# An attention and feed-forward kernel: V products of two key tiles in one batch, feed-forward products in small segments over double turns

## The chip, the core and the metric

The kernel runs on one NeuronCore of a Trainium2 chip. The metric is device time in microseconds (us) of one execution, the median of several runs. Five engines work side by side, each with its own instruction stream, and wait for each other by semaphores: TensorE (PE, matrix products; its weight loads are listed apart as PEld), VectorE (DVE), ScalarE (ACT), GpSimd (POOL) and SyncE (SP, which issues DMAs here).

## What is computed

The input is one sequence of 2048 tokens of width 512. After a layer norm, full attention with 32 heads of width 16 runs beside a gated feed-forward block of width 1792, and the two are joined:

```
xn = layernorm(x)
q, k, v = split(xn @ wqkv)                  # 32 heads of 16
p = softmax(q @ k.T / sqrt(16))             # 2048 x 2048 for each head
s = (p @ v) @ wo
h = (xn @ w_gate) * (xn @ w_up)
out = x + s * silu(h @ w_down)
```

All of it is in fp32. Most products are split in a high and a low part (fp32r), which gives three products for each one.

## The kernel before, in words

**Units and turns.** The attention is cut into 32 units `i` (8 groups of 4 heads, times 4 chunks of 512 queries). A unit takes 16 turns, one for each tile `kt` of 128 keys, so that there are 512 turns. A turn handles 4 heads `j`. For each head, `expo` (L568 to L578) makes the scores `t` (keys by queries, 128x512, one PSUM bank), and ScalarE takes their exponential into an SBUF tile `e`. Beside it `score` (L542) makes scores `s` of a later unit (queries by keys, `LEAD` = 21 turns ahead), whose row maxima VectorE takes (`mx`, L552). The maxima go back into `qs` by DMA and are subtracted by the product `t` itself.

**Couples.** `t` of head j uses the lower or the upper 64 rows of the PE array (its first row is 64 * (j % 2)), and `s` of head j ^ 1 the other 64 rows. The two run at the same time on the two halves; this text calls them a **couple**. A turn has four couples.

**V products.** `pv` (L580) multiplies the four `e` tiles with 32 columns of V each. The four products take all 128 rows and one column group of 32 each, and run at the same time; being fp32, each is carried out in two passes (8 matmul records for 4 products). This text calls what stands together a **batch**. Before, the batch of a turn is issued at the end of the next turn. All 16 turns of a unit add into one bank `pv`, which `finish` transposes and divides by its last column.

**Filler.** What PE does beside the attention comes from a generator, `filler` and later `ending`: products of q and k (`p`), gate and up (`g`, `u`), down (`y`) and the output (`z`). They come as `pair`s (L229): two outputs in two banks, one product on the lower 64 rows and one on the upper 64 rows at each step. This text calls one such step a **pair step**. One call of `pair` (a **call** below) makes 12 or 15 pair steps, exchanges the halves (between them ScalarE reads one word of the second bank, `look`, L251, for which the second half waits), and makes as many again. Calls of 24 pair steps are 13 of `p`, 56 of `g` and `u` and 8 of `y`; calls of 30 are 16 of `y`. That is 2328 pair steps (`SLOTS`), and the output's come on top. `Filler.part` (L758) is called once in each turn, after the second couple. It spreads each half of a call evenly over a number of turns that `spread` (L771) gives out of `FFN_ROUNDS` = 484, so that a turn has 4, 5 or 6 pair steps in one piece.

A turn on PE is thus: couple, couple, 4 to 6 pair steps, couple, couple, batch.

**Buffers.** PSUM has 8 banks (`BUFS`): 2 for `t` (tag st), 3 for `s`, 1 for `pv`, 2 for the filler (misc). So the third `t` may start only when the first one's exponential has read its bank: couple n waits for the exponential of couple n - 2, and for the maximum of couple n - 3. `e` has 12 buffers. The order on PE, ACT and DVE is the order of the code (`manual_schedule`); only DMAs and POOL are placed by the framework. `soon(n, f)` issues f after n more couples.

Of the kernel before, what the change touches and what calls it, by code (L numbers as in the profile page):

```python
# [21 lines left out]
NT = S // P  # L22
# [6 lines left out]
VW = DH + 1  # L29
VCOLS = (H - 1) * VW + 32  # L30
THIRDS = [range(0, 5), range(5, 10), range(10, 14)]
LEAD = 21
FFN_ROUNDS = 484
SLOTS = 24 * (NC * (NG // 2 - 1) + 1) + 36 * NF * NC
SPLIT_ROUNDS = 4
EBUFS = 12
# [10 lines left out]
def body(ctx, tc, x, wqkv, wo, wg, wu, wd, out):  # L47
    nc = tc.nc
# [3 lines left out]
    def dma(dst, src):  # L52
        nc.sync.dma_start(dst, src)
# [22 lines left out]
    V = keep.tile([P, NT, VCOLS], F32, name="V")  # L76
# [42 lines left out]
    def etile():  # L119
        return ep.tile([P, 512], F32, name="e", bufs=EBUFS)  # L120
# [398 lines left out]
    def load_q(i):  # L519
        g, c = divmod(i, NC)  # L520
        QS[i] = q = keep.tile([P, 2, 512], F32R, name="qs", bufs=3)
        MX[i] = keep.tile([P, 4, 4, 4], F32, name="mx", bufs=2)
        for e in range(2):
            dmar(q[64 * e:64 * e + KB], two(QD[g // 2][c][64 * (g % 2):64 * (g % 2) + 64], e))

    def load_k(g, cs=range(NC)):
        heads = slice(64 * (g % 2), 64 * (g % 2) + 64)
        for e in range(2):
            k = ks[g % 2][64 * e:64 * e + KB]
            if g < 2:  # L530
# [14 lines left out]
    def score(i, r, j):  # L545
        kc, t = divmod(r, 4)
        b, pr = 64 * (j % 2), j // 2
        k = ks[(i // NC) % 2]
        o = psum("s", f"s{i}_{r}_{j}")
        nc.tensor.matmul(o, QS[i][b:b + KB, pr, t * P:(t + 1) * P],  # L550
                         k[b:b + KB, pr, kc * 512:(kc + 1) * 512], start=True, stop=True)
        nc.vector.tensor_reduce(MX[i][:, j, t, kc:kc + 1], o, axis=AX.X, op=OP.max)  # L552
# [18 lines left out]
    def expo(i, kt, j):  # L571
        b, pr = 64 * (j % 2), j // 2
        k = ks[(i // NC) % 2]
        o = psum("st", f"t{i}_{kt}_{j}")
        nc.tensor.matmul(o, k[b:b + KR, pr, kt * P:(kt + 1) * P], QS[i][b:b + KR, pr], start=True, stop=True)  # L575
        e = etile()
        nc.scalar.activation(e, o, AF.Exp, scale=DH ** -0.5)  # L577
        return e  # L578

    def pv(i, kt, es):  # L580
        g = i // NC
        if kt == 0:
            fst["pv"] = psum("pv", f"pv{i}")
        for j in range(4):
            h0 = (4 * g + j) * VW
            nc.tensor.matmul(fst["pv"][32 * j:32 * j + 32], V[:, kt, h0:h0 + 32], es[j],  # L586
                             start=kt == 0, stop=kt == NT - 1)

    def finish(i):

        g, c = divmod(i, NC)
        tr = keep.tile([P, 16, 32], F32, name="tr", bufs=1)
        tn = tr.rearrange("p b e -> p (b e)")
        nc.vector.transpose(tn, fst["pv"])
# [121 lines left out]
    def filler(wq0):  # L716
        yield from proj_pair(0, [(wq0, 0, 2), (wq0, 0, 3)])
        for m in range(1, NG // 2):
            wk, wq = qk_weights(m, 1), qk_weights(m, 0)
            for c in range(NC):  # L720
                yield from proj_pair(m, [(wk, 1, c), (wq, 0, c)])
                if m == 1 and c:
                    after = fst["high"].ins.name
                    for n, src in enumerate((xh, xl)):
                        put = nc.sync.dma_start(XD[c][n].bitcast(F32), src[c].bitcast(F32))
                        tc.add_manual_dep(put.ins, after, BEHIND, reason="not before the first exponentials")
                if m == NG // 2 - 1 and c == NC - 2:
# [8 lines left out]
    heads = []  # L736

    def step_small(q):
        if q and next(q[0], 1):
            q.pop(0)  # L740

    class Filler:


        def __init__(self, gen, rounds):
            self.gen, self.rounds = gen, rounds
            self.left = self.parts = 0
            self.done = False

        def fetch(self):  # L750
            v = next(self.gen, self)
            if v is self:
                self.done = True
            elif v:
                self.left, self.parts = v[1], self.rounds(v[1])

        def part(self):
            if not self.left and not self.done:  # L758
                self.fetch()
            if self.left:  # L760
                n = -(-self.left // self.parts)
                for _ in range(n):
                    next(self.gen)
                self.left -= n
                self.parts = max(1, self.parts - 1)
                if not self.left:
                    self.fetch()

    cum = [0]

    def spread(n):  # L771
        a = cum[0]
        cum[0] += n
        return max(1, round(cum[0] * FFN_ROUNDS / SLOTS) - round(a * FFN_ROUNDS / SLOTS))

    prev = None
    with tc.manual_schedule(engines=ORDERED):
        with banks_of(EARLY_BUFS):
            fil = Filler(filler(early()), spread)
        ctx.enter_context(banks_of(BUFS))  # L780
        for n in range(NU * 16):
            now[0] = n
            i, kt = divmod(n, 16)
            g, c = divmod(i, NC)
            si, sr = divmod(n + LEAD, 16)
            if kt == 8 and i + 2 < NU:
                load_q(i + 2)
            if kt == 0 and g + 1 < NG and c == 1:
# [24 lines left out]
        run(finish(NU - 1))  # L813
        flush()
        last_heads()
        while fil.left or not fil.done:
            now[0] += 1
            prepare()
            fil.part()
            flush()  # L820
    ffp.close()

# [15 lines left out]
```

## Time and profile before

| | |
|---|---|
| time, median of 3 runs | 1816.01 us (1815.8 to 1816.85) |
| span of the profiled execution, first to last instruction | 1815.7 us; of its own time the record gives no more than this span |
| POOL busy | 580.7 us (32%) |
| PEld busy (weight loads, beside PE) | 991.1 us (55%) |
| DMA, mean over the span | 80 GB/s |

The span lies 0.3 us below the median of the runs. A busy share says little by itself here: PE's matmul records overlap, so that what a stretch costs is read from the starts of its records in the timeline, which is an answer of the trace that lists instructions in order of time: start, duration, engine, line, operation, output<-inputs, shapes, and how many records are merged. In square brackets stand the idle time of that engine before it and what ended it.

### The profile page before, as it was taken

What the parts mean: (1) busy time and instruction counts of PE and PEld (TensorE: products, weight loads), DVE (VectorE), ACT (ScalarE), POOL (GpSimd) and SP (SyncE); (2) the same over time, 40 slices, a digit from 0 to 9 for tenths busy, and PEclk for the clock granted to TensorE, in tenths of its full rate; (3) what the DMA queues carried; (4) which work ended last, traced back from release to release, by engine and by line L of the source; (5) the groups of instructions that cost most, each with busy time, mean ns of one, the idle gap of its engine ahead of it and who ended that gap; (6) DMA issues with size and microseconds to landing.
All of it is one profiled execution on the core that took longest, in us unless ns stands there. A gap on an engine that the chain in (4) does not pass through costs nothing.

```text
span 1815.7 us, 34194 instructions
## 1 busy us (share of the span) xinstructions
PE 1794.1 (99%) x13568; PEld 991.1 (55%) x13568; DVE 1474.4 (81%) x2456; ACT 1238.3 (68%) x2365; POOL 580.7 (32%) x647
## 2 busy tenths in 40 slices
PE   8899999999999999999999999999999999999998
PEld 5565555555555555555555555555555555555555
DVE  8488888888888888888888888888888888888832
ACT  5137676777776767777777777776767767767674
POOL 5321332431331325232132441431315323223441
PEclk9899999999999999999999999999999999999999
DMA  5424633520222122321115220411125111111352
GB/s 198 112 54 163 225 118 115 148 62 22 68 64 54 49 86 80 80 55 42 39 42 131 69 63 22 94 52 33 52 79 126 46 40 57 34 48 45 110 156 79
DMA packets 117227, 145.72 MB, mean 80 GB/s; under 512 B 12620, under 2 KB 74060, under 8 KB 114380
## 3 DMA queue, kind: packets, MB, share of 16 engines
q1 hardware_dynamic: 117068, 143.55, 27.7%
q8 instruction: 106, 1.74, 0.4%
q14 instruction: 53, 0.43, 0.1%
HBM read 95.94 MB, written 47.45 MB: 79 GB/s over the span
## 4 chain that ended last, share of the span: by engine, by line
PE 94%; DVE 2%; DMA 2%; POOL 1%; issue 0%; ACT 0%; SPq 0%; POOLq 0%; ACTq 0%; DVEq 0%
PE pv L586 27%; PE t L575 21%; PE s L550 11%; PE y L243 6%; PE u L243 5%; PE g L243 4%; PE u L247 4%; PE g L247 4%; PE y L247 3%; PE p L243 3%; PE v L224 2%; PE p L247 2%; PE z L243 1%; PE z L247 1%; DMA wdr<-in_wd_dram 1%; PE p L224 0%
## 5 line engine op out<-in xcount | busy, mean ns | idle before, releaser
L552 DVE TENSOR_REDUCE mx<-s 128x1 f32<-128x512 f32 x2048 | 1311.7, 683 | 268.5 <-PE s L550 162.7
L577 ACT ACTIVATE e<-t 128x512 f32<-128x512 f32 x2048 | 1111.9, 596 | 427.0 <-PE s L550 236.3
L550 PE MATMUL s<-ks,qs 48*128 48x512 f32 x2048 | 700.1, 427 | 10.0 <-DMA ks<-KD 8.8
L575 PE MATMUL t<-qs,ks 50*128 50x512 f32 x2048 | 705.2, 426 | 0.3 <-ACT e L577 0.3
L575 PEld LDWEIGHTS t<-qs,ks 50*128 50x128 f32 x2048 | 347.2, 185 | 499.4 <-ACT e L577 474.0
L586 PE MATMUL pv<-e,V 128*32 128x512 f32 x4096 | 545.7, 605 | 0.0
L550 PEld LDWEIGHTS s<-ks,qs 48*128 48x128 f32 x2048 | 337.4, 185 | 33.9 <-issue 12.9
L138 POOL CAST w0h<-w0r 128x512 fp32r<-128x512 f32 x60 | 36.7, 612 | 407.2 <-PE u L243 257.9
L586 PEld LDWEIGHTS pv<-e,V 128*32 128x32 f32 x4096 | 81.0, 108 | 156.5 <-issue 147.3
L352 POOL CAST dh<-wdr 128x512 fp32r<-128x512 f32 x56 | 33.8, 614 | 182.9 <-PE y L247 92.4
L247 PE MATMUL u<-fh,w0h 64*128 64x512 f32 x224 | 88.2, 394 | 0.1
L247 PE MATMUL y<-dh,hh 64*128 64x512 f32 x224 | 88.1, 393 | 0.0
L243 PE MATMUL u<-fh,w0l 64*128 64x512 f32 x224 | 88.0, 393 | 0.0
L243 PE MATMUL g<-fh,w1l 64*128 64x512 f32 x224 | 87.8, 392 | 0.0
L247 PE MATMUL g<-fl,w1h 64*128 64x512 f32 x224 | 87.8, 392 | 0.0
L243 PE MATMUL u<-fh,w0h 64*128 64x512 f32 x224 | 87.7, 392 | 0.0
L247 PE MATMUL g<-fh,w1h 64*128 64x512 f32 x224 | 87.7, 392 | 0.0
L243 PE MATMUL g<-fh,w1h 64*128 64x512 f32 x224 | 87.7, 391 | 0.0
L243 PE MATMUL u<-fl,w0h 64*128 64x512 f32 x224 | 87.6, 391 | 0.0
L243 PE MATMUL g<-fl,w1h 64*128 64x512 f32 x224 | 87.6, 391 | 0.0
L243 PE MATMUL y<-dh,hh 64*128 64x512 f32 x224 | 87.6, 391 | 0.0
L243 PE MATMUL y<-dl,hh 64*128 64x512 f32 x224 | 87.5, 391 | 0.0
(250 smaller groups left out, 2885.1 us busy)
## 6 DMA issues: line engine op xcount, KB each, us to landing
w1r<-in_wg_dram SPq DMA_DIRECT2D x56, 256.0 KB
w0r<-in_wu_dram SPq DMA_DIRECT2D x56, 256.0 KB
wdr<-in_wd_dram SPq DMA_DIRECT2D x56, 256.0 KB
qs<-QD SPq DMA_DIRECT2D x64, 192.0 KB
ks<-KD SPq DMA_DIRECT2D x12, 768.0 KB
KD<-hl SPq DMA_DIRECT2D x16, 512.0 KB
QD<-hl SPq DMA_DIRECT2D x16, 512.0 KB
OD<-tr SPq DMA_DIRECT2D x31, 256.0 KB
```

Source lines behind the costliest of these rows:

```text
L138: cast = nc.gpsimd.tensor_copy(hi, raw)
L224: nc.tensor.matmul(o, l(d), r(d), start=k == d == 0, stop=k == 2 and d == ND - 1)
L243: nc.tensor.matmul(outs[k], l[LOWER], r[LOWER], start=k == 0 and n == 0, stop=(stop or k == 0) and n == len(low) - 1, skip_group_check=k == 1)
L247: nc.tensor.matmul(outs[1 - k], l[UPPER], r[UPPER], start=k == 0 and m == 0, stop=(stop or k == 0) and m == len(high) - 1, skip_group_chec ...
L352: nc.gpsimd.tensor_copy(dh[:, i], raw)
L550: nc.tensor.matmul(o, QS[i][b:b + KB, pr, t * P:(t + 1) * P], k[b:b + KB, pr, kc * 512:(kc + 1) * 512], start=True, stop=True)
L552: nc.vector.tensor_reduce(MX[i][:, j, t, kc:kc + 1], o, axis=AX.X, op=OP.max)
L575: nc.tensor.matmul(o, k[b:b + KR, pr, kt * P:(kt + 1) * P], QS[i][b:b + KR, pr], start=True, stop=True)
L577: nc.scalar.activation(e, o, AF.Exp, scale=DH ** -0.5)
L586: nc.tensor.matmul(fst["pv"][32 * j:32 * j + 32], V[:, kt, h0:h0 + 32], es[j], start=kt == 0, stop=kt == NT - 1)
```

## The change

It does three things. `pv` takes the `e` tiles of two turns and issues 8 products in one batch (16 matmul records). The batch moves from the end of a turn to the middle of every even turn, after its second couple. And the filler is dealt out in segments: five in each double turn, one after the last couple of the even turn and one after each couple of the odd turn. A call of `pair` as a whole (both halves, 24 or 30 pair steps) gets a whole number of double turns, 2 to 4 out of `PHASES` = 242, and so 10, 15 or 20 segments. `finish` is issued two couples after the batch. Banks and buffers stay as they were.

```diff
-FFN_ROUNDS = 484
+PHASES = 242
+SEGS = 5
...
-    def pv(i, kt, es):
+    def pv(i, es):
         g = i // NC
-        if kt == 0:
-            fst["pv"] = psum("pv", f"pv{i}")
-        for j in range(4):
...
+        for kt, four in es:
+            if kt == 0:
+                fst["pv"] = psum("pv", f"pv{i}")
+            for j in range(4):
...
+                k, self.half = v
+                if not self.segs:
+                    self.total = self.left = self.half * (2 - k)
+                    self.segs = self.all = SEGS * self.phases(self.total)
...
+        def segment(self):
+            if not self.half and not self.done:
+                self.fetch()
+            if not self.segs:
+                return
+            self.segs -= 1
+            n = self.left - self.total * self.segs // self.all
+            self.left -= n
+            while n and not self.done:
+                if not self.half:
+                    self.fetch()
+                    continue
+                m = min(n, self.half)
+                for _ in range(m):
                     next(self.gen)
-                self.left -= n
-                self.parts = max(1, self.parts - 1)
-                if not self.left:
+                n -= m
+                self.half -= m
+                if not self.half:
                     self.fetch()
...
-        return max(1, round(cum[0] * FFN_ROUNDS / SLOTS) - round(a * FFN_ROUNDS / SLOTS))
+        return max(1, round(cum[0] * PHASES / SLOTS) - round(a * PHASES / SLOTS))
...
+    def products():
+        pv(*before)
+        if before[1][-1][0] == NT - 1:
+            i = before[0]
+
+            def rest():
+                heads.append(finish(i))
+                step_small(heads)
+            soon(2, rest)
...
-            es = []
+            four = []
+            es.append((kt, four))
             for j in range(4):
-                es.append(expo(i, kt, j))
+                four.append(expo(i, kt, j))
...
-                    fil.part()
+                if kt % 2 == 0 and j == 1 and before:
+                    products()
+                if kt % 2 or j == 3:
+                    fil.segment()
...
-            if prev is not None:
-                pv(*prev)
-                if prev[1] == NT - 1:
-                    heads.append(finish(prev[0]))
-                    step_small(heads)
-            prev = i, kt, es
-        pv(*prev)
+            if kt % 2:
+                before, es = [i, es], []
+        pv(*before)
+        flush()
...
-        while fil.left or not fil.done:
+        while not fil.done:
```

The order on PE around key tile 8 of unit 17, in names unit_tile_head: before, the last two couples of tile 7, the batch of tile 6, then the first two couples of tile 8 and the first of its pair steps.

```order
L575 MATMUL t17_7_2_14293<-qs_12780,ks0_132 128x512
L550 MATMUL s18_12_3_14297<-ks0_132,qs_13553 128x512
L575 MATMUL t17_7_3_14300<-qs_12780,ks0_132 128x512
L550 MATMUL s18_12_2_14304<-ks0_132,qs_13553 128x512
L586 MATMUL pv17_14019<-e_14198,V_137 32x512
...
L575 MATMUL t17_8_0_14315<-qs_12780,ks0_132 128x512
L550 MATMUL s18_13_1_14319<-ks0_132,qs_13553 128x512
L575 MATMUL t17_8_1_14322<-qs_12780,ks0_132 128x512
L550 MATMUL s18_13_0_14326<-ks0_132,qs_13553 128x512
L243 MATMUL g2_1_14283<-fl_13981,w1h_13991 128x512
```

After, on PE in the same place: the last couple of tile 7, a segment of one pair step, both couples of tile 8, the batch of tiles 6 and 7 (8 rows), and the third couple of tile 8.

```order
L576 MATMUL t17_7_3_14266<-qs_12772,ks0_132 128x512
L551 MATMUL s18_12_2_14270<-ks0_132,qs_13548 128x512
L244 MATMUL u2_0_14057<-fh_13997,w0l_13354 128x512
L248 MATMUL g2_0_14056<-fh_13997,w1l_13348 128x512
L576 MATMUL t17_8_0_14298<-qs_12772,ks0_132 128x512
L551 MATMUL s18_13_1_14302<-ks0_132,qs_13548 128x512
L576 MATMUL t17_8_1_14306<-qs_12772,ks0_132 128x512
L551 MATMUL s18_13_0_14310<-ks0_132,qs_13548 128x512
L588 MATMUL pv17_14033<-e_14192,V_137 32x512
...
L576 MATMUL t17_8_2_14321<-qs_12772,ks0_132 128x512
```

Before, a batch or a piece of filler of 4 to 6 pair steps stood between a couple and the second one after it. Now from `t17_7_3` to `t17_8_1`, two couples on in the same bank, there is one couple and one pair step.

On ACT before, the rows from tile 7 to tile 8 of the same unit: the copy `g` and the copy `hh` of the filler stand between exponentials of couples that have a batch or a piece of filler behind them.

```order
L577 ACTIVATE e_14205<-t17_6_1_14203 128x512
L346 ACTIVATE g_14222<-g2_0_14038 128x512
L577 ACTIVATE e_14243<-t17_6_2_14241 128x512
L577 ACTIVATE e_14251<-t17_6_3_14249 128x512
L577 ACTIVATE e_14264<-t17_7_0_14262 128x512
L577 ACTIVATE e_14271<-t17_7_1_14269 128x512
L306 ACTIVATE hh_13985<-h_14224 128x512
```

After, on ACT: `g` stands behind the last exponential of the odd turn, and `hh` behind the fourth of the even turn, so ahead of the first of the odd turn.

```order
L578 ACTIVATE e_14268<-t17_7_3_14266 128x512
L347 ACTIVATE g_14275<-g2_0_14056 128x512
L578 ACTIVATE e_14300<-t17_8_0_14298 128x512
L578 ACTIVATE e_14308<-t17_8_1_14306 128x512
L578 ACTIVATE e_14323<-t17_8_2_14321 128x512
L578 ACTIVATE e_14330<-t17_8_3_14328 128x512
L307 ACTIVATE hh_14002<-h_14277 128x512
L578 ACTIVATE e_14347<-t17_9_0_14345 128x512
```

Both copies moved from the middle of a turn to places around the batch.

On PE after, where a call's two halves meet within a double turn: the last pair step of the first half of `u2_0`, the couple with `t17_5_1`, and the first pair step of the second half, which exchanges the rows and waits for `look`.

```order
L244 MATMUL g2_0_14056<-fh_13997,w1l_13348 128x512
L248 MATMUL u2_0_14057<-fh_13997,w0l_13354 128x512
L576 MATMUL t17_5_1_14159<-qs_12772,ks0_132 128x512
L551 MATMUL s18_10_0_14163<-ks0_132,qs_13548 128x512
L244 MATMUL u2_0_14057<-fh_13997,w0h_13353 128x512
```

Before, the two halves were always in different turns, with two couples, a batch and two couples between them.

More of the change, by code (lines that the diff above doesn't have):

```diff
@@ L578, in expo @@
         return e
-    def pv(i, kt, es):
+    def pv(i, es):
         g = i // NC
-        if kt == 0:
-            fst["pv"] = psum("pv", f"pv{i}")
-        for j in range(4):
-            h0 = (4 * g + j) * VW
-            nc.tensor.matmul(fst["pv"][32 * j:32 * j + 32], V[:, kt, h0:h0 + 32], es[j],
-                             start=kt == 0, stop=kt == NT - 1)
+        for kt, four in es:
+            if kt == 0:
+                fst["pv"] = psum("pv", f"pv{i}")
+            for j in range(4):
+                h0 = (4 * g + j) * VW
+                nc.tensor.matmul(fst["pv"][32 * j:32 * j + 32], V[:, kt, h0:h0 + 32], four[j],
+                                 start=kt == 0, stop=kt == NT - 1)
     def finish(i):
@@ L742, in body, with __init__ @@
     class Filler:
-        def __init__(self, gen, rounds):
-            self.gen, self.rounds = gen, rounds
-            self.left = self.parts = 0
+        def __init__(self, gen, phases):
+            self.gen, self.phases = gen, phases
+            self.half = self.left = self.total = self.gone = self.segs = 0
             self.done = False
@@ L754, in fetch @@
             elif v:
-                self.left, self.parts = v[1], self.rounds(v[1])
-        def part(self):
-            if not self.left and not self.done:
-                self.fetch()
-            if self.left:
-                n = -(-self.left // self.parts)
-                for _ in range(n):
+                k, self.half = v
[4 more added lines that the diff above has]
+            if not self.half and not self.done:
+                self.fetch()
+            if not self.segs:
[9 more added lines that the diff above has]
+                for _ in range(m):
                     next(self.gen)
-                self.left -= n
-                self.parts = max(1, self.parts - 1)
-                if not self.left:
+                n -= m
+                self.half -= m
+                if not self.half:
                     self.fetch()
@@ L773, in spread @@
         cum[0] += n
-        return max(1, round(cum[0] * FFN_ROUNDS / SLOTS) - round(a * FFN_ROUNDS / SLOTS))
-    prev = None
+        return max(1, round(cum[0] * PHASES / SLOTS) - round(a * PHASES / SLOTS))
+    before, es = [], []
+    def products():
[6 more added lines that the diff above has]
+            soon(2, rest)
     with tc.manual_schedule(engines=ORDERED):
@@ L815, in body @@
         last_heads()
-        while fil.left or not fil.done:
+        while not fil.done:
             now[0] += 1
             prepare()
-            fil.part()
+            fil.segment()
             flush()
```

## The prediction

> **What bounds the kernel now.** I read the page first (busy shares, clock, chain), then the costliest groups, then the timeline of single turns.
>
> ```profile
> PE 1794.1 (99%) x13568; PEld 991.1 (55%) x13568; DVE 1474.4 (81%) x2456; ACT 1238.3 (68%) x2365; POOL 580.7 (32%) x647
> ...
> PEclk9899999999999999999999999999999999999999
> ...
> PE 94%; DVE 2%; DMA 2%; POOL 1%; issue 0%; ACT 0%; SPq 0%; POOLq 0%; ACTq 0%; DVEq 0%
> ...
> L552 DVE TENSOR_REDUCE mx<-s 128x1 f32<-128x512 f32 x2048 | 1311.7, 683 | 268.5 <-PE s L550 162.7
> L577 ACT ACTIVATE e<-t 128x512 f32<-128x512 f32 x2048 | 1111.9, 596 | 427.0 <-PE s L550 236.3
> ```
>
> PE is 94% of the chain of waits at a full clock: it never waits long, and what it saves ends the kernel sooner. But DVE and ACT, which must clear the banks behind it, are at 81% and 68%. A turn with four pair steps, in order of time (start, duration):
>
> ```profile
> 700.72 0.61 PE L586 MATMUL pv<-e,V 128*32 128x512 f32 x4
> ...
> 701.27 0.50 PE L575 MATMUL t<-qs,ks 50*128 50x512 f32 x1
> ...
> 701.61 0.40 PE L575 MATMUL t<-qs,ks 50*128 50x512 f32 x1
> ...
> 701.80 1.09 ACT L577 ACTIVATE e<-t 128x512 f32<-128x512 f32 x2 [0.61 <-PE t L575]
> ...
> 701.84 0.40 PE L247 MATMUL g<-fl,w1h 64*128 64x512 f32 x1
> ...
> 702.08 0.40 PE L247 MATMUL g<-fh,w1l 64*128 64x512 f32 x1
> ...
> 702.55 0.39 PE L247 MATMUL g<-fl,w1h 64*128 64x512 f32 x1
> ...
> 702.78 0.40 PE L575 MATMUL t<-qs,ks 50*128 50x512 f32 x1
> ...
> 702.94 0.18 PEld L575 LDWEIGHTS t<-qs,ks 50*128 50x128 f32 x1 [0.20 <-ACT e L577]
> ...
> 703.02 0.42 PE L575 MATMUL t<-qs,ks 50*128 50x512 f32 x1
> 703.22 1.08 ACT L577 ACTIVATE e<-t 128x512 f32<-128x512 f32 x2 [0.33 <-PE s L550]
> 703.37 0.16 PEld L586 LDWEIGHTS pv<-e,V 128*32 128x32 f32 x8 [0.24 <-issue]
> 703.37 1.06 PE L586 MATMUL pv<-e,V 128*32 128x512 f32 x8
> 704.37 0.50 PE L575 MATMUL t<-qs,ks 50*128 50x512 f32 x1
> ```
>
> From start to start: a pair step takes 0.23 us (701.84 to 702.08), a couple 0.24 (702.78 to 703.02), and the second couple behind a batch comes 0.34 after the first (701.27 to 701.61). The batch begins 0.33 behind the last couple and takes 1.00; its second pass starts 0.55 before the next couple (700.72, 701.27), so its first takes 0.45. An exponential starts 0.44 after its score (702.78, 703.22), behind a batch 0.53 (701.27, 701.80), and the second of two 0.49 after the first (1.09 less the 0.60 of one). The turn takes 3.10. With five and six pair steps:
>
> ```profile
> 901.45 0.50 PE L575 MATMUL t<-qs,ks 50*128 50x512 f32 x1
> ...
> 903.75 1.07 PE L586 MATMUL pv<-e,V 128*32 128x512 f32 x8
> 904.75 0.49 PE L575 MATMUL t<-qs,ks 50*128 50x512 f32 x1
> ...
> 1702.84 0.50 PE L575 MATMUL t<-qs,ks 50*128 50x512 f32 x1
> ...
> 1706.35 0.50 PE L575 MATMUL t<-qs,ks 50*128 50x512 f32 x1
> ```
>
> That is 3.30 and 3.51. Two turns take 6.20, 6.60 and 7.02 with 8, 10 and 12 pair steps.
>
> **What goes.** One batch of four passes replaces two of two. Bounds: 2 x 1.00 if PE runs empty between the key tiles, 3 x 0.45 + 0.55 = 1.90 if the passes follow as the first two do. I take 1.90, since the eight weight loads of a batch (703.37, 0.16 long) are done while its first pass runs, so that a later pass finds its weights loaded. That saves 0.10. One entry goes (0.33 less the 0.23 of an undisturbed step, 0.10) and one exit (0.34 less 0.23, 0.11). Together 0.31 in a double turn, and with 256 of them 79 us, if nothing waits.
>
> The Trainium skill ("TensorE: Matmul & The Clock Gate", Part 3 on packing small matmuls) says that a weight load overlaps running matmuls only where its row group differs. Both key tiles of a batch use all rows, so by that rule the second would load only behind the first, and the batch would stay at its upper bound. The row of 703.37 speaks against it: the loads of the second pass, in the same rows, are done long before the first pass ends.
>
> **What comes.** Scores now stand closer together, with only two banks for `t`. What a bank costs is seen where the trace has no batch or filler between couples, at the first change of turns:
>
> ```profile
> 118.38 0.40 PE L575 MATMUL t<-qs,ks 50*128 50x512 f32 x1
> ...
> 118.84 0.39 PE L575 MATMUL t<-qs,ks 50*128 50x512 f32 x1
> 119.03 2.48 DVE L552 TENSOR_REDUCE mx<-s 128x1 f32<-128x512 f32 x4 [0.73 <-PE s L550]
> 119.48 0.18 PEld L575 LDWEIGHTS t<-qs,ks 50*128 50x128 f32 x1 [0.69 <-ACT e L577]
> 119.48 0.50 PE L575 MATMUL t<-qs,ks 50*128 50x512 f32 x1 [0.26 <-ACT e L577]
> ...
> 119.97 0.49 PE L575 MATMUL t<-qs,ks 50*128 50x512 f32 x1
> ...
> 120.31 0.39 PE L247 MATMUL p<-xh,w0h 64*128 64x512 f32 x1
> ```
>
> A score comes 1.10 (118.38, 119.48) and 1.13 (118.84, 119.97) after the second one before it, PE stands idle, and what follows such a late score is 0.34 behind it (119.97, 120.31), not 0.23. So a couple starts no earlier than 1.10 after the couple before the last; where that one is the first behind a batch, 1.20 (0.53 for 0.44); where it is the second, 1.34, since its exponential waits for the first's.
>
> I walk a double turn from the first couple behind the batch, A at 0, B at 0.34; C to F belong to the odd turn, G and H to the next even one, then the batch. A couple behind n pair steps comes 0.23 (n + 1) after the one before. The segments along the new order on PE come to 114 double turns with 2, 2, 1, 2, 1 pair steps, 42 with 2 each, 92 with 3, 2, 3, 2, 2 (the output's among them) and 8 others.
>
> - **8 pair steps:** C is due at 1.03, but its bank is free at 1.20. D 1.89, E 2.35, F 3.04, G 3.50. H is due at 3.74, free at F + 1.10 = 4.14: a wait of 0.40 with PE empty. The batch starts 0.33 + 0.10 later at 4.57 and ends at 6.47. Before: 6.20. **+0.27 each, +31 us.**
> - **10:** C 1.20, D 1.89, E 2.58, F 3.27, G 3.96; H due 4.20, free 4.37; batch 4.70, end 6.60. Before: 6.60. **0.**
> - **12:** C 1.26, D 1.95, E 2.87, F 3.56, G 4.25; H due 4.49, free 4.66; batch 4.99, end 6.89. Before: 7.02. **-0.13 each, -12 us.** The 8 others: about +1.
>
> So the waits at C and H eat the 79 us and 20 more. To these come the filler's own evictions, which lay beside long stretches before:
>
> ```profile
> L306 ACT ACTIVATE hh<-h 128x512 fp32r<-128x512 f32 x56 | 35.5, 633 | 0.0
> ...
> L251 ACT ACTIVATE look<-u 1x1 f32<-1x1 f32 x56 | 9.0, 160 | 15.5 <-PE u L247 12.6
> ...
> L594 DVE STREAM_TRANSPOSE tr<-pv 128x512 f32<-128x512 f32 x32 | 22.9, 714 | 1.9 <-PE pv L586 1.9
> ```
>
> - **`look`:** calls of three double turns have their middle inside one. Of 24 pair steps there are 38 (114 / 3), with one couple between the halves; of 30 there are 14 (42 / 3), with none. The last product before the middle ends 0.40 after its start, `look` takes 0.16, and with 0.14 for two hand-overs (estimated: of the 1.10 and 1.13 above, 0.44 and 0.60 taken off leave 0.06 and 0.09 for one) the second half starts 0.70 after it, for 0.46 and 0.23 planned: 38 x 0.24 + 14 x 0.47 = **16 us**.
> - **`hh`** now runs ahead of C's exponential: 0.63 behind B's, so that C's ends some 0.4 late and E waits 0.35 where there are 8 pair steps; about half of the 56: **10 us**. With 12, E is late enough. `g` and `h` come behind G, where the batch covers them: 0; without that cover 0.6 x 56 = 34.
> - **DVE:** four reductions in a row take 2.48, less 0.68 over three 0.60 each; eight are 4.8, and the rest of DVE's work (1474.4 - 1311.7 over 256) is 0.6: 5.4 of 6.47, with the batch to catch up in. `tr`, 0.71 once in a unit, now stands ahead of C's reduction: 31 x 0.35 = 11 at most, 0 at least; I take **5**.
>
> POOL's and SP's work keeps its place relative to the filler's calls; the weights' lead is a whole call, which spans two or three double turns of 6 to 7 us, so nothing is counted. The tail behind the last batch keeps its order.
>
> **Sum.** 1815.7 + 20 + 16 + 10 + 5 = 1866.7; the span is 0.3 below the median: **1867 us**, 2.8% slower.
>
> How well the loop is counted by these turns: `t` runs from 116.3 to 1798.1, so a double turn takes 6.57 on average, between the 6.20 and 7.02 of the walks.
>
> ```profile
> L575 PE MATMUL t<-qs,ks x2048: 386/397/502, 116.3 to 1798.1; 50*128 50x512 f32 x187
> ```
>
> **Rivals.**
> 1. *Faster: the waits stay small.* If H and C find their banks free, 79 us go: 1737; with half of the waits and of the 31 us, about 1805. It decides at 0.31 of waits in a double turn. For it: nearly all of PE's short waits today are hidden, as at 702.94, where a load 0.20 late cost 0.01. Against it: 119.48, where PE is idle, and H needs the bank 0.70 or 0.93 after F, less than 1.10.
> 2. *The batch saves nothing inside* (PE empty between key tiles, 2.00): 0.10 x 256 = 26 more: 1893. Against it stand the early loads.
> 3. *DVE falls behind:* some 110 transposes and additions of 0.7 land between reductions of the odd turn and each makes a score wait 0.35 for one of three banks: 38 more: 1905. For it: 5.4 of 6.47; against it: the 1.9 of the batch, in which DVE catches up.
> 4. *Even:* bank waits 0.1 shorter and no cost from the filler's evictions: 20 - 20 = 0: 1816.
>
> **Chances.** Forecast (1830 to 1890) 0.69; faster 0.15; batch 0.05; DVE 0.07; even 0.04. A difference under 0.2% cannot be told from none here. The range leaves out the faster case and the far end of the DVE case: 1820 to 1905, that is, no `look`, `hh` or `tr` cost and bank waits slightly shorter at the low end, and both upper bounds of the unknown costs at the high end. Slower 0.81, within 0.2% 0.04, faster 0.15.
>
> **What would show it.** The row of PE's weight load `t` waiting for ACT `e`: today its 474 us lie behind batches; I expect PE itself idle before `t` for a sum near 60 us or more, above all at heads 0 and 1 of even turns. Double turns of 8 pair steps near 6.5 and of 12 near 6.9; the batch near 1.9; ACT's share falling with the span. Wrong would be: PE's idle below 20 us, or a batch that takes 2.0.

## The result, and the profile after

| | before | after |
|---|---|---|
| time, median of 4 runs each on one chip | 1815.9 us (1814.14 to 1816.85) | 1891.26 us (1890.1 to 1892.32) |
| ratio, with its 95% interval | | 1.0412 (1.0398 to 1.0427) |
| span of the profiled execution | 1815.7 us | 1890.3 us |

The change makes the kernel 4.1% slower. The predicted sign and mechanism held. The 1891 us lie inside the range of 1820 to 1905, but 24 us above the predicted 1867, 1 us above the upper end of the forecast itself (1830 to 1890), and nearest to the 1893 of the second rival. That rival needs a batch of 2.00 us; the batch takes 1.86 here (below). The page of after has these two rows: the busy time of each engine and the chain of waits.

```profile
PE 1837.7 (97%) x13568; PEld 1010.0 (53%) x13568; DVE 1473.7 (78%) x2456; ACT 1259.1 (67%) x2365; POOL 578.4 (31%) x647
...
PE 89%; ACT 6%; DVE 2%; DMA 1%; issue 1%; POOL 0%; SPq 0%; ACTq 0%; POOLq 0%; DVEq 0%
```

PE still looks 97% busy, yet the chain runs through ACT for 6% of the span, some 113 us, where it was 0% before. DVE's busy time stood still and ACT's rose by 21 us, so their shares fell with the longer span. The groups of after show why "PE busy" is no measure here (busy, mean ns of one, then the idle time before them and what ended it):

```profile
L576 PE MATMUL t<-qs,ks 50*128 50x512 f32 x2048 | 842.1, 433 | 22.5 <-ACT e L578 18.2
...
L576 PEld LDWEIGHTS t<-qs,ks 50*128 50x128 f32 x2048 | 357.1, 184 | 486.7 <-ACT e L578 302.8
...
L551 PEld LDWEIGHTS s<-ks,qs 48*128 48x128 f32 x2048 | 350.3, 184 | 35.0 <-issue 13.1
```

Matmul ends are modelled, and they are drawn long enough to cover most gaps: only 18.2 us of PE's idle time goes to `e`, while the same 13568 matmuls take 43.6 us more of "busy" (1837.7 - 1794.1). What waits is the weight load of `t`, for the exponential that frees its bank; the load of `s` waits for nearly nothing. (The other 152.9 us ahead of the load of `t` are listed under "issue".) The loop as a whole tells how much: its `t` rows of before ran from 116.3 to 1798.1, and now

```profile
L576 PE MATMUL t<-qs,ks x2048: 387/399/503, 116.0 to 1872.1; 50*128 50x512 f32 x187
```

which is 1756.1 for 1681.8: all of the 74 us lies in the loop. One double turn of 8 pair steps, first on PE alone (A at 246.56, C, the pair step behind C, D, E, F, G, H, the batch, and the next A):

```profile
246.56 0.50 PE L576 MATMUL t<-qs,ks 50*128 50x512 f32 x1
...
247.75 0.50 PE L576 MATMUL t<-qs,ks 50*128 50x512 f32 x1
...
248.09 0.39 PE L244 MATMUL p<-xh,w0h 64*128 64x512 f32 x1
...
248.56 0.39 PE L576 MATMUL t<-qs,ks 50*128 50x512 f32 x1
...
249.02 0.41 PE L576 MATMUL t<-qs,ks 50*128 50x512 f32 x1
...
249.74 0.40 PE L576 MATMUL t<-qs,ks 50*128 50x512 f32 x1
...
250.22 0.40 PE L576 MATMUL t<-qs,ks 50*128 50x512 f32 x1
250.82 0.50 PE L576 MATMUL t<-qs,ks 50*128 50x512 f32 x1 [0.20 <-ACT e L578]
...
251.25 1.93 PE L588 MATMUL pv<-e,V 128*32 128x512 f32 x16
253.11 0.50 PE L576 MATMUL t<-qs,ks 50*128 50x512 f32 x1
```

C comes 1.19 after A and H 1.08 after F (249.74): the two places that the walk named, at the times that it gave (1.20 and 1.10). Three things differ from it. Behind the late C the next step comes 0.34 later (248.09), not 0.23, which the walk applied only behind H; the batch takes 1.86, not 1.90; and the whole is 6.55, not 6.47. With 12 pair steps (F, G, H, batch, next A):

```profile
833.41 0.40 PE L576 MATMUL t<-qs,ks 50*128 50x512 f32 x1
834.10 0.39 PE L576 MATMUL t<-qs,ks 50*128 50x512 f32 x1
834.50 0.50 PE L576 MATMUL t<-qs,ks 50*128 50x512 f32 x1
834.93 1.92 PE L588 MATMUL pv<-e,V 128*32 128x512 f32 x16
836.79 0.50 PE L576 MATMUL t<-qs,ks 50*128 50x512 f32 x1
```

H waits here too (0.40 behind G, 1.09 behind F), and the batch follows 0.43 later, where the walk had 0.33. Taken from the starts of `t` over the whole trace, from one A to the next (before: from the third couple of a turn to the third couple two turns on), the mean lengths are:

| pair steps | before: number, us | after: number, us | undisturbed after | walked in the prediction |
|---|---|---|---|---|
| 8 | 82, 6.23 | 118, 6.74 | 6.55 | 6.47 |
| 10 | 111, 6.63 | 42, 7.06 | 6.76 | 6.60 |
| 12 | 50, 7.03 | 89, 6.98 | 6.97 to 7.02 | 6.89 |

"Undisturbed" gives the usual length of those without a wait for `look` or `hh`. A few double turns with other numbers of pair steps are left out. The longest are those with 10 pair steps and the exchange of the halves in their middle. These rows of after show one: PE and ACT at its second half.

```profile
921.45 0.40 PE L244 MATMUL y<-dh,hl 64*128 64x512 f32 x1
...
921.71 0.60 ACT L578 ACTIVATE e<-t 128x512 f32<-128x512 f32 x1 [0.18 <-PE t L576]
922.20 0.14 ACT L252 ACTIVATE look<-y 1x1 f32<-1x1 f32 x1
...
922.40 0.50 PE L244 MATMUL y<-dh,hh 64*128 64x512 f32 x1 [0.50 <-ACT look L252]
```

`look` stands behind an exponential of 0.60, so that the second half starts 0.95 after the last product of the first (921.45, 922.40); the prediction had 0.70.

### The profile page after: what moved, and what is told of

Same layout as the page of the kernel before. It is cut to its first block, busy times and chain, and to the rows that moved or that the text cites. A ratio compares the mean times of both kernels' runs of the same rounds, so it can differ in the third digit from the quotient of the medians.

```text
span 1890.3 us, 34219 instructions
## 1 busy us (share of the span) xinstructions
PE 1837.7 (97%) x13568; PEld 1010.0 (53%) x13568; DVE 1473.7 (78%) x2456; ACT 1259.1 (67%) x2365; POOL 578.4 (31%) x647
## 4 chain that ended last, share of the span: by engine, by line
PE 89%; ACT 6%; DVE 2%; DMA 1%; issue 1%; POOL 0%; SPq 0%; ACTq 0%; POOLq 0%; DVEq 0%
PE pv L588 25%; PE t L576 23%; PE s L551 10%; PE u L244 7%; ACT e L578 6%; PE g L244 5%; PE y L244 5%; PE y L248 3%; PE p L244 2%; PE u L248 2%; PE z L244 2%; PE v L225 2%; PE g L248 1%; PE p L248 1%; PE p L225 0%
## 5 line engine op out<-in xcount | busy, mean ns | idle before, releaser
L578 ACT ACTIVATE e<-t 128x512 f32<-128x512 f32 x2048 | 1156.1, 598 | 536.3 <-PE s L551 337.0
L576 PE MATMUL t<-qs,ks 50*128 50x512 f32 x2048 | 842.1, 433 | 22.5 <-ACT e L578 18.2
L551 PE MATMUL s<-ks,qs 48*128 48x512 f32 x2048 | 830.1, 435 | 10.9 <-DMA ks<-KD 8.8
L576 PEld LDWEIGHTS t<-qs,ks 50*128 50x128 f32 x2048 | 357.1, 184 | 486.7 <-ACT e L578 302.8
L588 PE MATMUL pv<-e,V 128*32 128x512 f32 x4096 | 492.5, 598 | 0.0
L551 PEld LDWEIGHTS s<-ks,qs 48*128 48x128 f32 x2048 | 350.3, 184 | 35.0 <-issue 13.1
L588 PEld LDWEIGHTS pv<-e,V 128*32 128x32 f32 x4096 | 107.0, 109 | 215.6 <-issue 212.7
L308 POOL TENSOR_TENSOR hl<-h,hh 128x512 fp32r<-128x512 f32 x56 | 72.3, 1291 | 74.6 <-ACT hh L307 74.5
L248 PE MATMUL g<-fh,w1h 64*128 64x512 f32 x224 | 91.3, 408 | 0.0
L248 PE MATMUL g<-fh,w1l 64*128 64x512 f32 x224 | 88.2, 394 | 0.0
L244 PE MATMUL u<-fh,w0l 64*128 64x512 f32 x224 | 88.1, 393 | 0.0
L248 PE MATMUL u<-fh,w0l 64*128 64x512 f32 x224 | 88.1, 393 | 0.0
L244 PE MATMUL g<-fh,w1l 64*128 64x512 f32 x224 | 87.9, 393 | 0.0
```

The source lines that it names most:

```text
L244: nc.tensor.matmul(outs[k], l[LOWER], r[LOWER], start=k == 0 and n == 0, stop=(stop or k == 0) and n == len(low) - 1, skip_group_check=k == 1)
L248: nc.tensor.matmul(outs[1 - k], l[UPPER], r[UPPER], start=k == 0 and m == 0, stop=(stop or k == 0) and m == len(high) - 1, skip_group_chec ...
L308: nc.gpsimd.tensor_tensor(lo, h, hi, op=OP.subtract)
```

## Experiments

The **bank theory** says: the gain of the joined batch is real, and what eats it is the round trip of the two `t` banks (score, exponential, next score) wherever couples stand too close, above all from A to C and from F to H. Its rivals were that the joined batch itself gains nothing or brings the loss, that DVE is the limit, and that small segments as such cost. All times are medians beside runs of the kernel before on the same chip.

### 1. The batch taken apart

The segments and places of after, but one key tile in each batch, behind the second couple of every turn.

```diff
-                if kt % 2 == 0 and j == 1 and before:
+                if j == 1 and before:
                     products()
...
-            if kt % 2:
-                before, es = [i, es], []
+            before, es = [i, es], []
```

> Undoes the batch of two alone: segments as in the change, but a batch of one key tile behind the second couple of every turn. Bank theory (couples wait for the exponential that frees the bank of `t`; the batch of two itself is a gain): the batch costs 2 x 1.00 for 1.85, one entry and one exit more, some 0.36 us in each of 256 double turns, less a part of the waits of the odd turn, which the second batch covers: 1950 to 1980 us. Rival (a batch of two saves nothing, PE runs empty between the key tiles): 1890 or less, since the waits of the odd turn fall.

Measured: 1961.45 us, ratio 1.0802 (1.0784 to 1.082). Joining the batches is worth 70 us where the segments are small, or 0.27 in each of 256 double turns, against the 0.31 of the prediction. Some 8 us of the 70 have another cause: with a batch in every turn, the first batch of a unit waits for `tr`, which has to read the bank of the unit before (after has no such wait; experiment 8 takes this up):

```profile
PE pv L588 <- DVE tr L596: 7.9, 30, 0.6
```

Without them 0.24 is left. The rival falls: the joined batch isn't the loss.

### 2. More and smaller segments

Seven segments, behind every couple but the one ahead of the batch, so that one stands between G and H.

```diff
-SEGS = 5
+SEGS = 7
...
-                if kt % 2 or j == 3:
+                if (kt % 2 or j != 1) and n + j:
                     fil.segment()
```

> The change with seven segments in a double turn for five: one behind each couple but the one ahead of the batch, the same pair steps in all. Bank theory: couples stand farther apart where they now stand together (A from B, G from H), so waits at C and H shrink by 0.1 to 0.3 in a double turn: 1825 to 1870 us. Rival (each piece of filler costs PE something when it changes between scores and filler, 75 us for the three pieces that a double turn has more than before, 0.1 each): two pieces more, 1940 us.

Measured: 1874.56 us, 1.032 (1.0303 to 1.0337): 17 us better than after, but 5 above the expected range. By its trace the double turns of 10 and 12 pair steps gain (6.75 and 6.89 for 7.06 and 6.98), while those of 8 stay at 6.73. With 8, none of the layouts with a joined batch that were tried here came down to the 6.23 of before.

### 3. Three banks for `t`, two for `s`

```diff
-BUFS = {"st": 2, "s": 3, "pv": 1, "misc": 2}
+BUFS = {"st": 3, "s": 2, "pv": 1, "misc": 2}
```

> The change with three banks for `t` and two for `s` in place of two and three. Bank theory: PE's waits for the exponential nearly vanish, and PE waits for the maxima instead, whose bank is held 0.44 + 0.69 us and which run one behind the other at 0.60: the time does not fall below 1885 and may rise to 1950, with the waits of the loads of `s` on DVE above 100 us. Rival (banks do not matter, the pieces themselves cost): 1891 within 5, and few waits of either kind.

Measured: 1964.09 us, 1.0819 (1.0796 to 1.0843), 14 above the expected range. The groups of weight loads show the wait changing hands:

```profile
L576 PEld LDWEIGHTS t<-qs,ks 50*128 50x128 f32 x2048 | 359.3, 185 | 255.3 <-issue 214.4 <-ACT e L578 0.2
L551 PEld LDWEIGHTS s<-ks,qs 48*128 48x128 f32 x2048 | 349.7, 184 | 217.7 <-DVE mx L553 186.0 <-issue 12.9
```

With a third bank `t` waits 0.2 us for ACT in place of 302.8, and `s`, now with two, waits 186.0 for DVE. (The 214.4 us under "issue" are 256 waits, one for each batch.) So what `t` waits for is its bank, and how many there are decides it. The eight banks can't give three to both. That this split is the worse one is put down to the slower reduction (a mean of 683 ns for 598 of the exponential in after); this was not tested apart.

### 4. `hh` two couples earlier

```diff
-                    soon(4, lambda h=h, hi=hh[:, i], lo=hl[:, i]: hidden(h, hi, lo))
+                    soon(2, lambda h=h, hi=hh[:, i], lo=hl[:, i]: hidden(h, hi, lo))
```

> The change with the copy `hh` issued two couples after its product, behind H's exponential and beside the batch, in place of four. Bank theory with the prediction's term: 10 us go, 1881 us; at most 20 if the copy delays more couples than E. Rival (the copy is hidden): 1891 within 3.

Measured: 1885.36 us, 1.0378 (1.0362 to 1.0394): 6 us better than after, for 10 expected. The copy does stand in the way where the change put it, at a little over half of the price in the prediction.

### 5. Shorter exponentials, with and without the change

The exponential alone is shortened, in the changed kernel and, as a control, in the kernel before. Both leave out half of each exponential: it covers the first 256 columns of the bank. The edit is the same in both; the tiles `e` become persistent, with their other half set to 1 once.

```diff
-        nc.scalar.activation(e, o, AF.Exp, scale=DH ** -0.5)
+        nc.scalar.activation(e[:, 0:256], o[:, 0:256], AF.Exp, scale=DH ** -0.5)
```

> The change with exponentials over the first 256 columns of each bank only; the other half of each e tile is set to 1 once at the start and left (half of the exponentials is left out; products, maxima and filler are all there). A row of 512 takes 0.60, one of a single word 0.16, so half a bank should take about 0.38, and the bank of `t` comes free 0.22 earlier. Bank theory: C no longer waits, H waits 0.2 at most, the double turns of 8, 10 and 12 pair steps take about 6.0, 6.3 and 6.7, and the change becomes a gain: 1745 to 1785, 30 to 65 us below e6. Rival (the pieces of filler cost PE something of their own): it stays some 75 us above e6.

> The kernel before with the same half exponentials, as the control of e5. Both theories: nearly the time of before, since only its turns of 4 pair steps wait for a bank, by 0.05: 1800 to 1818.

Measured: 1803.42 us with the change, 0.9922 (0.9903 to 0.9942), and 1806.64 without it, 0.9936 (0.9915 to 0.9956). By the ratios the kernel before gains 0.6% (12 us), and the changed one 4.9% of the time of before (1.0412 to 0.9922, 89 us). The change, which costs 75 us with full exponentials, comes out at -3 with short ones. The length of the exponential is thus the cause of some 78 us. By itself this doesn't tell the bank from a busy ACT; experiment 3 does, where a third bank ends the wait for ACT with exponentials of full length. But a gain of 30 to 65 on the control was expected, and 1745 to 1785 us: that part was missed. The weight load's waits, after and with the short exponentials (engine, line, waited for: us, times, longest):

```profile
PEld t L576 <- ACT e L578: 302.8, 801, 0.8
```
```profile
PEld t L584 <- ACT e L586: 105.2, 411, 0.6
```

A third of the waiting is left. An exponential now takes 0.384, 0.21 less, so the round trip is still about 0.89, and with 8 pair steps H is due 0.70 after F. Those double turns take 6.11 undisturbed and 6.35 on average, for 6.18 in the control; `look`, in their middle, is not shortened at all (6.40 for the 34 that wait for it alone). In 16 others the load of `s` waits for VectorE, and they take 6.86:

```profile
PEld s L559 <- DVE mx L561: 20.1, 56, 1.1
```

With 12 pair steps hardly anything waits, and there the change gives 6.73 for 7.03 (by the medians 6.77 for 7.03): 0.26 to 0.30, most of the 0.31. The expectation had forgotten H, `look` and the reductions.

### 6. Fewer and larger pieces

Two pieces in a double turn (behind the last couple of each turn), and three (behind B, D and F), with the joined batch:

```diff
-SEGS = 5
+SEGS = 2
...
-                if kt % 2 or j == 3:
+                if j == 3:
```
```diff
-SEGS = 5
+SEGS = 3
...
-                if kt % 2 or j == 3:
+                if (kt % 2 and j == 1) or j == 3:
```

> The change with the batch of two kept and the segments undone: one piece of filler in a turn, behind its last couple, so that four couples stand together in the odd and the next even turn. Bank theory: of four couples in a row the third and fourth wait 0.6 and 0.8 with PE empty: a double turn of 10 pair steps takes 7.2, 1940 to 1980 us. Rival (pieces cost PE): three pieces fewer than in the change, back to 1740 to 1816.

> The change with three pieces of filler in a double turn for five, behind the couples B, D and F, so couples in twos as before the change. Bank theory: the waits move from C and H to C, D, F and H and sum to about the same: 1880 to 1905. Rival (pieces cost PE, 0.1 each): two fewer, 1840.

Measured: 1969.62 us, 1.0839 (1.0818 to 1.0861), and 1893.76, 1.042 (1.04 to 1.0441), both inside what was expected. With two pieces the four couples C to F stand in a row, and the time is the worst of all. So the joined batch needs filler between the couples, and used in every double turn it stays above before with two, three, five and seven pieces. But by double turns the three pieces are already better than before with 12 pair steps, 6.84 for 7.03, and worse with 8, 6.89 for 6.23. That the total was met is in part luck: about 0.27 of the 0.66 lost with 8 is no wait for a bank of `t`, but `look`. The double turns of 8 that wait for nothing else take 6.57 at the median, and the 38 that wait for `look` 7.41, as PE stands still for it:

```profile
PE u L244 <- ACT look L252: 14.6, 28, 1.0
PE y L244 <- ACT look L252: 11.4, 18, 0.7
```

The 6.57 is still 0.34 above before.

### 7. The segments alone

One key tile in a batch at the end of each turn, as before, with six segments in a double turn.

```diff
-                if kt % 2 == 0 and j == 1 and before:
-                    products()
-                if kt % 2 or j == 3:
+                if j < 3:
                     fil.segment()
...
-            if kt % 2:
-                before, es = [i, es], []
+            if before:
+                products()
+            before, es = [i, es], []
```

> The second half of the change alone: batches of one key tile at the end of each turn, as before, and the filler in six segments in a double turn, behind the first, second and third couple of each turn. Bank theory: in a turn with four pair steps the second couple behind a batch now comes 0.34 + 2 x 0.23 = 0.80 after the first, and the fourth needs its bank, 1.20 later: 2.00, with 0.33 and 1.00 for the batch 3.33 a turn, 6.66 a double turn for 6.20 before. With six pair steps (two behind each couple) the fourth is due at 2.18 and hardly waits: 7.0 to 7.1 as before. With 82 double turns of 8, 111 of 10 and 50 of 12 pair steps in the trace of before that is 82 x 0.46 + 111 x 0.2 = 60 us: 1860 to 1905 us. Rival (small segments are harmless by themselves, only what stands around the joined batch waits): 1805 to 1830.

Measured: 1925.65 us, 1.0597 (1.0581 to 1.0613): far outside the rival's 1805 to 1830, and 20 above the expected range. A turn with four pair steps goes as worked out (first couple behind a batch, second, third, fourth, batch):

```profile
953.98 0.49 PE L576 MATMUL t<-qs,ks 50*128 50x512 f32 x1
...
954.78 0.39 PE L576 MATMUL t<-qs,ks 50*128 50x512 f32 x1
...
955.50 0.39 PE L576 MATMUL t<-qs,ks 50*128 50x512 f32 x1
...
955.95 0.41 PE L576 MATMUL t<-qs,ks 50*128 50x512 f32 x1
956.29 0.64 PE L588 MATMUL pv<-e,V 128*32 128x512 f32 x4
```

The second is at 0.80, the fourth at 1.97 (2.00 worked out), the batch at 2.31. What the expectation lacked is seen in the trace. Double turns without any other wait take 6.64, 6.63 and 7.09 with 8, 10 and 12 pair steps, much as worked out. But with 12 the mean is 7.33: 23 of them hold a wait of a call's first products for `h` (L349) and take 7.42, six hold one for `y` (L374) and take 8.00, four at the end wait for VectorE's work on the output (L418) and take 8.5 to 10.8. In 20 places the batch waits for `tr`.

```profile
PEld u L248 <- DVE h L349: 10.1, 43, 0.6
PE y L248 <- DVE y L374: 3.2, 8, 0.5
PE pv L588 <- DVE tr L596: 7.0, 20, 0.5
```

All of these are reads of a bank by VectorE, for which the next products in it wait. Taken as what lies above the undisturbed lengths, such waits make up some 50 of the 108 us, an estimate; no run took them out one by one. So the segments alone are dear, and only in part by the banks of `t`.

### 8. Each layout where it fits

If the theory is right, a joined batch should be used only where a double turn has 12 pair steps. The mixture puts a call of two double turns in the layout of three pieces, and all others in one like that of before, half a turn on (one key tile behind the second couple and one piece of filler behind the last one of each turn).

```diff
-SEGS = 5
+PLACES = {2: ((0, 3), (1, 1), (1, 3)), 3: ((0, 3), (1, 3))}
...
-                    self.segs = self.all = SEGS * self.phases(self.total)
+                    phases = self.phases(self.total)
+                    self.places = PLACES.get(phases, PLACES[3])
+                    self.segs = self.all = len(self.places) * phases
...
-                if kt % 2 == 0 and j == 1 and before:
+                if j == 1 and es and (kt % 2 == 0 or fil.places is not PLACES[2]):
                     products()
-                if kt % 2 or j == 3:
+                if (kt % 2, j) in fil.places:
                     fil.segment()
```

> A mixture by the number of pair steps in a double turn. Where a call gets two double turns (12 pair steps each, 88 or so double turns): a batch of two key tiles and three pieces of filler, behind the second, fourth and sixth couple. Elsewhere (8 or 10 pair steps): a batch of one key tile in each turn and one piece of filler in each turn, two couples from a batch on both sides, as before. Bank theory: from the first couple behind a batch to the last ahead of the next, six exponentials of 0.60 follow a first score of 0.53, so a joined batch of 1.85 with 0.33 ahead of it costs at least 0.53 + 3.6 + 0.06 + 0.33 + 1.85 = 6.37 a double turn, while single batches allow 2 x (0.53 + 1.2 + 0.06 + 0.33 + 1.0) = 6.24; the work itself is more than either with 12 pair steps. So the joined batch gains where there are 12 and loses where there are 8. From the traces: 118 double turns of 8 at 6.22, 42 of 10 at 6.62 (as before), 89 of 12 at 6.85 (three pieces), 6 others at 6.4: 1660 us for the loop's 255 double turns, 1676 before: 1800 us, 1793 to 1810, 0.3 to 1.2% faster than before. Rival (the loss comes from something else that a joined batch brings, whatever stands around it, or from the change of layout itself): 1816 or more.

Measured: 1812.57 us, 0.9973 (0.9962 to 0.9983), 0.3% faster than before, though 3 us above the expected range. The double turns of 12 and 10 are as expected (6.86 and 6.66). Those of 8 have a median of 6.20 but a mean of 6.31, and the waits name what is late:

```profile
PE pv L588 <- DVE tr L596: 8.5, 20, 0.6
```

`finish` is issued two couples behind the batch, as in the change; where a batch stands in every turn, the next unit's first one is then held up by `tr`, which must first read the bank. So `finish` goes back to its place right behind the batch there:

```diff
-            soon(2, rest)
+            if fil.places is PLACES[2]:
+                soon(2, rest)
+            else:
+                rest()
```

> The mixture by the number of pair steps once more, but where batches hold one key tile, the transpose that reads the bank of the V products is issued right behind a unit's last batch, as before the change, and not two couples later. In the mixture's trace the next unit's first batch, now only four couples behind, waited for that transpose (20 times), and the 17 double turns of 8 pair steps in which this happened took 6.72 in place of 6.20. If the late transpose is their cause, 17 x 0.52 = 9 us go: 1799 to 1808 us, 0.5 to 1.0% faster than before. Rival (those double turns are long because a unit begins in them, whatever the transpose does): 1810 to 1815, 0.1 to 0.4% faster.

Measured: 1804.46 us, 0.9929 (0.9915 to 0.9942). The wait is gone, 8 us of the 9 with it, and this version beats both kernels, that of before by 0.7%. Its page and one double turn of 12 (A, B, then C with D, E with F, G with H, each two merged in a row, the batch, the next A):

```profile
PE 1780.1 (99%) x13568; PEld 995.1 (55%) x13568; DVE 1473.7 (82%) x2456; ACT 1235.4 (69%) x2365; POOL 579.8 (32%) x647
...
PE 93%; DVE 2%; POOL 2%; DMA 1%; issue 1%; ACT 1%; SPq 0%; ACTq 0%; POOLq 0%; DVEq 0%
```
```profile
930.79 0.50 PE L576 MATMUL t<-qs,ks 50*128 50x512 f32 x1
931.12 0.43 PE L576 MATMUL t<-qs,ks 50*128 50x512 f32 x1
932.32 0.67 PE L576 MATMUL t<-qs,ks 50*128 50x512 f32 x2
933.81 0.65 PE L576 MATMUL t<-qs,ks 50*128 50x512 f32 x2
935.24 0.63 PE L576 MATMUL t<-qs,ks 50*128 50x512 f32 x2
935.80 1.92 PE L588 MATMUL pv<-e,V 128*32 128x512 f32 x16
937.66 0.50 PE L576 MATMUL t<-qs,ks 50*128 50x512 f32 x1
```

ACT is back to 1% of the chain. A pair of couples comes every 1.4 to 1.5 us with four pair steps between, longer than the round trip of its bank: 6.87. The control uses single batches there too, with one piece of filler in each turn as elsewhere:

```diff
-PLACES = {2: ((0, 3), (1, 1), (1, 3)), 3: ((0, 3), (1, 3))}
+PLACES = {3: ((0, 3), (1, 3))}
...
-                if j == 1 and es and (kt % 2 == 0 or fil.places is not PLACES[2]):
+                if j == 1 and es:
                     products()
```

> The control to the mixture: the same placing of calls on whole double turns, the batch behind the second couple of every turn, but one key tile in every batch and one piece of filler in every turn, also where a double turn has 12 pair steps. If the mixture's gain is the joined batch where there are 12, those 89 double turns go back from 6.86 to the 7.05 of before and the time is 17 us above the mixture's 1804.5: 1815 to 1826 us, within 0.5% of before. Rival (the gain is from the call's placing or from the half turn by which the batch moved): 1800 to 1808.

Measured: 1827.17 us, 1.0067 (1.0053 to 1.0081), 23 above the version with joined batches, for 17 expected and just above the expected range. The double turns of 12 go back to 7.03 (89 x 0.17 = 15 us), those of 8 from 6.24 to 6.29 (118 x 0.05 = 6). So the gain is the joined batch with its three pieces, at the place where the scores around it hardly wait.

## Why the prediction was right, and where its size was off

**What goes: right.** 0.31 in a double turn was predicted; experiment 1 gives 0.24 to 0.27, and experiment 5 gives 0.26 to 0.30 with 12 pair steps. Inside the batch the saving was larger than assumed: 1.86 for 1.90. By the rule of the Trainium skill ("TensorE: Matmul & The Clock Gate", Part 3) that was weighed there it would be 2.00, an estimate from 1.00 for a single batch; the trace doesn't agree. The second rival falls with it, though its 1893 us lies closer to the 1891 measured than the 1867 of the forecast does.

**What comes: right in kind and place.** The bank rule names C and H, and both stand there in the trace at the predicted distances. Experiment 3 shows that the wait is for the bank, experiment 5 that the exponential's length sets it, and experiments 6 and 8 that the joined batch pays or costs by the amount of filler between couples.

**The mis-sized term is the restart.** The prediction counted 0.34 for 0.23 behind a late score only at H with 8 pair steps. The prediction had shown the 0.34 itself, at 119.97. It holds at the other late scores too: behind C with 8 and 10, behind H with 10 and 12. Over the loop of after the batch starts 0.43 behind a late H at the median, and a pair step follows a late score by 0.33 to 0.34, also at the median. Since H hangs on F and F on C, each such 0.11 goes to the end of the double turn. Against the walk the undisturbed double turns are longer by 0.08 (8), 0.16 (10) and 0.09 (12, by the mean), the shorter batch included: 114 x 0.08 + 42 x 0.16 + 92 x 0.09 = 24 us, as much as lies between the 51 predicted and the 75 measured. That it fits so closely is in part luck, since the rest of the sum is not exact either: the walk took before at 6.20, 6.60 and 7.02, up to 0.03 below its means, and the evictions came out somewhat dearer.

**The filler's evictions: near in sum, wrong in parts, so the sum is luck.** The means of after lie above the undisturbed lengths by 118 x 0.19 + 42 x 0.30 = 35 us, for 31 predicted. By the starts of `t`, `look` costs 0.28 where one couple stands between the halves (0.24 predicted), but 0.8 where none does (0.47), since it stands behind an exponential; with 14 of those that is 5 us more. Of the 10 us put down to `hh`, its earlier place gave 6 back. `tr` was put ahead of C's reduction with 5 us; it was not tested apart in the changed kernel.

**DVE does not fall behind.** The load of `s` waits 35.0 us in all and only 8.2 of them for DVE:

```profile
PEld s L551 <- DVE mx L553: 8.2, 20, 1.0
```

That rival falls. **Faster** would have needed waits below 0.31 in a double turn: this happens with 12 pair steps and three pieces, and not with 8.

**The sign to look for was ill chosen.** The prediction asked for 60 us of PE's own idle time ahead of `t`, and called less than 20 a refutation. The row shows 18.2 us, although the mechanism is there: modelled ends of matmuls hide the gaps. The starts of the rows and the chain's 6% of ACT show it, idle time doesn't.

## What to carry to other kernels

Before a batch is joined, work out what must come between two of them: here six exponentials behind the first score, 0.53 + 6 x 0.60 + 0.06, then 0.33 and 1.86 make about 6.38 us in a double turn, an estimate from these rows, more than the 6.23 that the old order took with 8 pair steps and less than its 7.03 with 12. A saving on the bounding engine is worth its full price only where that engine has enough other work to stand between the uses of a bank, so choose the layout by the amount of that work, stretch by stretch. Ask too what else the freed order moves: here one read of a bank (`tr`) cost 8 us in the mixture, which in the end gains 12. And judge waits of PE by the starts of its instructions, from one iteration to the next.

## What was unexpected of the hardware

- Four passes of two key tiles (16 matmul records) take 1.86 us, less than 3 x 0.45 + 0.55 from the row of a single batch.
- After a wait that leaves PE empty, the first matmul is recorded with 0.50 us and the next step starts 0.34 later, not 0.23. In these traces this is 0.11 on top of the wait, even of a short one: H in the row of 834.50 was late by only 0.17, and the batch behind it by 0.10 more.
- Exponentials shorter by 0.21 took 12 us from the kernel before, where ACT is 68% busy, and 89 us from the changed one, where it is 67% busy: the share said nothing of what ACT's speed is worth.
